# An attention and mixer kernel with every engine's order written out, conversions in thirds, and a tiny weight in place of a repair

## The chip, the cores and the metric

One core of one Trainium2 chip. The metric is device time in microseconds (us) of one execution. Ratios are the mean time of one kernel's fast runs over the mean of the other's of the same rounds, so they are not quite the ratio of the medians that are quoted.

Engines: PE is TensorE, DVE is VectorE, ACT is ScalarE, POOL is GpSimd. "L371" is line 371 of the kernel that a profile belongs to. "Half clock" is a stretch in which the trace shows a granted TensorE clock of 0.5; "the lock" or "the port" is what DVE and POOL share (the prediction shows it); a bank is a piece of the memory that PE writes its products to. Names in the profiles: hp is the product of the hash and g its bits, sc the scores, e their exps, esa and esd the sums of exps made by POOL and DVE, sums their total on PE, den the reciprocal, XT the output of attention, trp its transposes and x their copies, t the products of the token mixer.

## The reference

```python
# attention: batch 4, heads 8, sequence 768, head dimension 64; proj is 64 x 6
q_bits = (q @ proj > 0); k_bits = (k @ proj > 0)           # six bits each: a bucket
scores = where(bucket(q) == bucket(k), q @ k.T / 8, -1e9)
attn   = softmax(scores); x = attn @ v                      # heads joined: x is 4 x 768 x 512
# mixer; the four weights come as float64
h  = relu(x.T @ w_tok1) @ w_tok2 ; u = x + h.T              # over the sequence
h2 = relu(u @ w_ch1) @ w_ch2     ; out = u + h2             # over the channels
```
A query with no key in its bucket gets, by the softmax of equal scores, the mean of all values.

## The kernel before

The program has three parts: attention (16 pairs of heads, each in two halves of the queries), a token mixer and a channel mixer. PE's order is that of the source; the order of all other engines is chosen by a scheduler. PE adds the masking term by a second product of hash bits, so a query without equal keys gets exps of zero and a sum of zero, which is repaired after the sums.

```python
# conversion of 128 x 768 float64 words to float32: lo and hi are the two halves
raw = pool.tile([P, NW, 2], U32, ..., bufs=3); nc.sync.dma_start(out=raw, in_=src)
nc.vector.tensor_scalar(big, hi, 3, 0x3FFFFFFF, op0=shift_left, op1=and)          # L138
nc.vector.scalar_tensor_tensor(big, hi, 0xC0000000, big, op0=and, op1=or)         # L142
nc.vector.tensor_scalar(unit, big, 0xFF800000, None, op0=and)                     # L147
nc.vector.scalar_tensor_tensor(unit, lo, 2.0**-52, unit, op0=mult, op1=mult)      # L150
nc.gpsimd.tensor_tensor(big, big, unit, op=add)                                   # L151
nc.gpsimd.tensor_tensor(size, hi, hi, op=mult)                                    # L154
nc.vector.scalar_tensor_tensor(to, size, LEAST*LEAST, big, op0=is_ge, op1=mult)   # L155
# ...
def collect(es):                       # sum of the six exps of a half
    a = es[0] + es[1]; a = a + es[2]                 # POOL, L265, L266
    d = es[3] + es[4]; d = d + es[5]; d = d + a      # DVE, L268 to L270
def divide(n, half, num, es):
    # sums = ones @ es                                 PE, L278
    none = (sums == 0)                               # DVE, L280
    den = none * S + sums                            # DVE, L282
    den = 1 / den                                    # DVE, L285
    num = none * vsum + num                          # DVE, L286
    XT = num * den                                   # POOL, L290
# ...
for n, half, g in groups:
    es = scores(n, half, ...)                        # PE L232, ACT exp L249
    if held is not None: step(held)                  # weigh (PE L257), divide, collect
    if half == 0 and g == 0:
        load(n + 3); look(n + 1)                     # look: range read, DVE L195
    if half == 1 and g == 0 and n % 2 == 1: hashes(n + 1)   # for two pairs
    if weights and n >= 2 and half == 0 and g == 1: weights.pop(0)()   # one conversion
# token mixer: turn (transposes), mix1 (L440), mix2 (L452, adds into XT L458);
# 16 of the 20 conversions stand here, four before each batch
```

## Time and profile before

| | before |
|---|---|
| median of three runs | 1014.91 us |
| span of the profiled run | 1008.7 us |
| attention, from the first weighing's end to the first mixer product | 26.9 to 403.4 us |
| token mixer, to the first channel product | 403.4 to 508.9 us |
| channel mixer and end | 508.9 to 1008.7 us |

### The profile page before, as it was taken

How to read it: one execution, taken by the hardware profiler on the slowest of the kernel's cores; microseconds unless marked ns; L12 is line 12 of the kernel's file. 1: busy time of each engine (PE TensorE's matmuls, PEld its weight loads, DVE VectorE, ACT ScalarE, POOL GpSimd, SP SyncE). 2: the span in 40 equal slices, each digit the busy share in tenths (PEclk: the TensorE clock that was granted, in tenths of full speed). 3: DMA queues.
4: the chain of work that ended last, by engine and by line, in shares of the span. 5: the costliest groups of instructions: out<-in, count | busy, mean ns of one | idle time of the engine just before them, and what ended most of it. 6: DMA issues, size and time to landing. Idle time of an engine off the chain costs nothing.

```text
span 1008.7 us, 9010 instructions
## 1 busy us (share of the span) xinstructions
PE 943.9 (94%) x3649; PEld 423.4 (42%) x3649; DVE 400.3 (40%) x425; ACT 240.7 (24%) x361; POOL 223.6 (22%) x153
## 2 busy tenths in 40 slices
PE   5838999999999998989799999999999999999997
PEld 1313443444344344544444444444444444444443
DVE  2787778879787867566660000000000000000000
ACT  3404554554455455210011001001001101100100
POOL 4533533443344443444330000000000000000000
PEclk9968999999999999989899999999999999999999
DMA  6502221321121002223210000000000000000000
GB/s 231 209 1 67 79 98 34 98 81 63 66 63 52 18 2 94 95 94 94 94 32 0 21 21 1 20 22 0 11 21 10 1 31 11 0 21 21 1 11 33
DMA packets 16912, 48.52 MB, mean 48 GB/s; under 512 B 2080, under 2 KB 2528, under 8 KB 16864
## 3 DMA queue, kind: packets, MB, share of 16 engines
q1 hardware_dynamic: 16864, 47.88, 13.8%
q8 instruction: 30, 0.49, 0.2%
q14 instruction: 18, 0.15, 0.0%
HBM read 40.90 MB, written 6.29 MB: 47 GB/s over the span
## 4 chain that ended last, share of the span: by engine, by line
PE 69%; DVE 17%; POOL 6%; DMA 3%; issue 3%; ACT 2%; SPq 1%; DVEq 0%; POOLq 0%; ACTq 0%
PE c L466 25%; PE c L476 25%; PE sc L232 10%; PE acc L257 7%; POOL tmp L151 3%; POOL raw L154 2%; DVE den L285 2%; DVE tmp L150 2%; DMA qk<-in_qk 2%; DVE tmp L142 2%; ACT e L249 1%; DVE esd L269 1%; DVE esd L268 1%; PE sums L278 1%; PE hp L207 1%
## 5 line engine op out<-in xcount | busy, mean ns | idle before, releaser
L466 PE MATMUL c<-XT,WC 128*128 128x512 f32 x576 | 248.3, 592 | 0.6 <-DVE XT L458 0.6
L476 PE MATMUL c<-r,WC 128*128 128x512 f32 x576 | 248.2, 592 | 0.0
L480 DVE TENSOR_TENSOR o<-c,XT 128x512 f32<-128x512 f32 x24 | 16.6, 692 | 458.8 <-PE c L476 458.8
L249 ACT ACTIVATE e<-sc 128x768 f32<-128x768 f32 x192 | 151.9, 809 | 141.6 <-PE sc L232 141.1
L232 PE MATMUL sc<-qk 64*128 64x384 f32 x768 | 168.9, 519 | 0.6 <-ACT e L249 0.6
L466 PEld LDWEIGHTS c<-XT,WC 128*128 128x128 f32 x576 | 109.4, 190 | 138.4 <-issue 137.0
L476 PEld LDWEIGHTS c<-r,WC 128*128 128x128 f32 x576 | 109.4, 190 | 137.8 <-issue 137.8
L471 ACT ACTIVATE r<-c 128x512 f32<-128x512 f32 x72 | 43.0, 597 | 441.4 <-PE c L466 441.4
L257 PE MATMUL acc<-e,vn 128*64 128x384 f32 x768 | 137.9, 494 | 0.0
L265 POOL TENSOR_TENSOR esa<-e 128x768 f32<-128x768 f32 x32 | 59.2, 1851 | 181.2 <-ACT e L249 181.2
L232 PEld LDWEIGHTS sc<-qk 64*128 64x128 f32 x768 | 68.1, 194 | 71.5 <-issue 60.5
L257 PEld LDWEIGHTS acc<-e,vn 128*64 128x64 f32 x768 | 49.5, 136 | 76.4 <-issue 75.5
L285 DVE RECIPROCAL den<-den 128x384 f32<-128x384 f32 x32 | 81.5, 2545 | 0.0
L232 PE MATMUL sc<-bits 64*128 64x384 bf16 x384 | 65.4, 328 | 1.9 <-DMA bits<-g 1.9
L266 POOL TENSOR_TENSOR esa<-esa,e 128x768 f32<-128x768 f32 x32 | 60.8, 1901 | 0.1
L151 POOL TENSOR_TENSOR tmp<-tmp 128x768 f32<-128x768 f32 x20 | 36.7, 1836 | 89.8 <-DVE tmp L150 89.8
L268 DVE TENSOR_TENSOR esd<-e 128x768 f32<-128x768 f32 x32 | 39.1, 1223 | 33.5 <-ACT e L249 33.3
L207 PE MATMUL hp<-qk,projblk 128*32 128x384 f32 x128 | 19.0, 628 | 34.0 <-DVE g L211 14.9
L452 PE MATMUL t<-W,r 128*128 128x384 f32 x128 | 43.8, 501 | 7.5 <-DVE XT L458 7.5
L440 PE MATMUL t<-x,W 128*128 128x512 f32 x96 | 43.5, 610 | 0.6 <-DVE XT L458 0.6
L290 POOL TENSOR_TENSOR XT<-num,den 128x384 f32<-128x384 f32 x32 | 33.4, 1043 | 32.5 <-DVE den L285 29.5
L195 DVE TENSOR_REDUCE largest<-qk 128x1 f32<-128x1536 f32 x16 | 27.7, 1730 | 29.8 <-DMA qk<-in_qk 29.8
(46 smaller groups left out, 464.6 us busy)
## 6 DMA issues: line engine op xcount, KB each, us to landing
qk<-in_qk SPq DMA_DIRECT2D x16, 768.0 KB
raw<-in_moe_w_ch SPq DMA_DIRECT2D x16, 768.0 KB
vn<-in_v SPq DMA_DIRECT2D x16, 384.0 KB
vt<-in_vT SPq DMA_DIRECT2D x16, 384.0 KB
out<-o SPq DMA_DIRECT2D x24, 256.0 KB
raw<-in_moe_w_tok SPq DMA_DIRECT2D x4, 768.0 KB
bits<-g SPq DMA_DIRECT2D x64, 10.5 KB
projblk<-in_proj SPq DMA_DIRECT2D x2, 1.5 KB
```

The lines of the kernel that those rows point to most:

```text
L151: nc.gpsimd.tensor_tensor(big, big, unit, op=ALU.add)
L232: nc.tensor.matmul(sc[c][:, i, :HALF], t[rows, 1, P * c : P * c + P], t[rows, 0, qs], start=first, stop=not first,)
L249: nc.scalar.activation(e, sc[c][:, :, :HALF], ACT.Exp, scale=SCALE)
L257: nc.tensor.matmul(acc[D * i : D * i + D, :HALF], vn[:, i, c], e[:, i], start=(c == 0), stop=(c == NR - 1),)
L265: nc.gpsimd.tensor_tensor(a, es[0], es[1], op=ALU.add)
L266: nc.gpsimd.tensor_tensor(a, a, es[2], op=ALU.add)
L268: nc.vector.tensor_tensor(d, es[3], es[4], op=ALU.add)
L285: nc.vector.reciprocal(den, den)
L440: nc.tensor.matmul(ps, W1[:, r, P * j : P * j + P], x[:, r], start=(r == 0), stop=(r == NR - 1),)
L452: nc.tensor.matmul(ps[:, :HALF], r1[:, j, P * cb : P * cb + P], W2[:, j, HALF * half : HALF * half + HALF], start=(j == 0), stop=(j == NJ ...
L466: nc.tensor.matmul(ps, WC1[:, cb, P * t : P * t + P], XT[:, cb, sl], start=(cb == 0), stop=(cb == NCB - 1),)
L476: nc.tensor.matmul(ps, WC2[:, t, P * cb : P * cb + P], r2[t], start=(t == 0), stop=(t == NHT - 1),)
```

## The change

Its intent: PE shall not wait for DVE. The repair is gone: every key gets a weight of 2^-82 in the sums, by the values' sum in the copy of the weighed values and by a constant in the last add. The range read moves into the channel part. A conversion is cut in three pieces, one in each half. Two of its operations go to ACT. The order of all engines is that of the source.

```diff
 class Conversion:
+    def begin(self):                                  # first third
+        nc.scalar.activation(lo.bitcast(F32), lo, ACT.Copy, scale=2.0**-52)       # L162
         nc.vector.tensor_scalar(big, hi, 3, 0x3FFFFFFF, ...)                      # L164
         nc.vector.scalar_tensor_tensor(big, hi, 0xC0000000, big, ...)             # L167
+    def join(self):                                   # middle third
         nc.vector.tensor_scalar(unit, big, 0xFF800000, ...)                       # L179
-        nc.vector.scalar_tensor_tensor(unit, lo, 2.0**-52, unit, ...)
+        nc.scalar.activation(hi, hi, ACT.Square)                                  # L182
+        nc.gpsimd.tensor_tensor(unit, unit, lo, op=ALU.mult)                      # L183
         nc.gpsimd.tensor_tensor(big, big, unit, op=ALU.add)                       # L184
-        nc.gpsimd.tensor_tensor(size, hi, hi, op=ALU.mult)
+    def end(self):                                    # last third: DVE, L193
+    def one(self):  # mixer: begin and join of this conversion, end of the one before, next fetch

 def divide(...):
-    none = ...; den = ...; num = ...
+    nc.vector.reciprocal(den, ps[:, :HALF])                                       # L322

+for n in range(len(pairs)):
+    for half in range(2):
+        now.scores(0)
+        if before: before.weigh(1)
+        if half == 0:
+            load(n + 2)
+            if n + 1 < len(pairs): hashes(n + 1)       # DVE L265, L266
+        if before: before.add(0)                       # DVE L367, L368
+        now.scores(1)
+        if half == 0 and n + 1 < len(pairs): add_values(n + 1)
+        if n:
+            weights.some(third); third = (third + 1) % 3
+        now.weigh(0)                                   # POOL esa L355
+        if before: before.add(1); before.divide()      # DVE L370, L371; PE sums L320; POOL XT L324
+        before = now
+# 8 conversions in attention, 12 in the mixer:
 def mix1(b):
+    if b or not first: turn(b, x, banks)               # transposes L223, copies to x on ACT L224
     for j in range(NJ):
         ...                                            # products L513, relu on ACT L516
+        weights.one()
 def mix2(b):
     for cb in range(NCB):
         ...                                            # products L526, adds into XT on DVE L532
+        if cb % 2: weights.one()
+# bits buffers 4 -> 3, qk buffers 4 -> 3; mixer banks 8 -> 4, with two pairs of banks for transposes
```

## The prediction

> **What bounds the kernel now.** I read the page first, then who waited for whom on PE, then the timelines of PE, DVE and POOL, and the order in which the changed program's instructions stand on each engine.
>
> ```profile
> PE 943.9 (94%) x3649; PEld 423.4 (42%) x3649; DVE 400.3 (40%) x425; ACT 240.7 (24%) x361; POOL 223.6 (22%) x153
> ...
> PE   5838999999999998989799999999999999999997
> ...
> DVE  2787778879787867566660000000000000000000
> ```
> PE is the bound. From slice 20 on DVE is idle and PE full: that is the channel part.
>
> ```profile
> 508.94 41.47 PE c L466 x96
> 550.41 41.20 PE c L476 x96
> ```
> Twelve such pieces take 508.9 to 1003.6 us, 41.2 each, without a gap. The change cannot shorten them. All gain must come from the first 509 us.
>
> ```profile
> PE hp L207 <- DVE g L211: 14.9, 8, 5.1
> PE hp L207 <- DVE den L282: 10.6, 1, 10.6
> PE sums L278 <- DVE den L282: 8.3, 1, 8.3
> PE t L452 <- DVE XT L458: 7.5, 1, 7.5
> ```
> There PE waits for DVE: 8.3 + 10.6 + 5.1 us between 46 and 80 us, where the weight conversions stand ahead of the sums of exps in DVE's queue; some 9 us more at later hashes; 7.5 us in the token mixer, where 16 conversions hold up the adds into XT.
>
> ```profile
> 101.85 2.62 PE sc L232 x18
> 104.47 2.09 PE acc L257 x12
> 106.56 0.65 PE sums L278 x4
> 107.20 2.62 PE sc L232 x18
> 109.82 2.09 PE acc L257 x12
> 111.91 2.62 PE sc L232 x18
> ```
> Undisturbed, one half of a pair is 2 x (2.62 + 2.09) + 0.65 = 10.07 us of PE. There are 32 halves. A hash without its wait adds 0.78.
>
> **What the Trainium skill says.** "SBUF — State Buffer", section "Who interferes with whom": a DVE instruction with two SBUF inputs and a GpSimd instruction that reads SBUF exclude each other; the later one blocks until the other is done. The trace agrees:
>
> ```profile
> 335.52 0.96 DVE L268 TENSOR_TENSOR esd<-e 128x768 f32<-128x768 f32 x1
> 336.58 1.57 DVE L269 TENSOR_TENSOR esd<-esd,e 128x768 f32<-128x768 f32 x1
> ...
> 335.63 1.70 POOL L290 TENSOR_TENSOR XT<-num,den 128x384 f32<-128x384 f32 x1 [2.96 <-DVE den L285]
> 337.30 2.51 POOL L266 TENSOR_TENSOR esa<-esa,e 128x768 f32<-128x768 f32 x1
> ```
> Alone these take 0.96, 0.96, 1.00 and 1.81 us. Here they alternate: each waits out the one before.
>
> "TensorE: Matmul & The Clock Gate", section "What's actually happening": the clock falls to half after an idle window of about 3.4 us, and windows run freely. The trace agrees only in part: gaps of 2.26 us (at 166 and 255 us) already cost about 1.5 us of half-speed matmuls, one of 2.47 us (at 344) cost none, and gaps under 0.7 none.
>
> "DMA: Bandwidth & Descriptors", section "Queues, rings and completion order": a queue's descriptors are consumed in ring order. The trace fits: bits issued from 14.9 us land only after the big loads queued first, which keep the DMA busy to about 14.2 us.
>
> **The change, part by part.**
>
> Start. Now the first hash needs pair 0 alone (before: pairs 0 and 1, the second landing at 9.9 us). The hash ends near 7 us. The first bits follow 3.9 MB of loads in the same queue, and at the roughly 400 GB/s that the DMA moved early, they land near 13.5 us instead of 18.6. Behind them come, at the half clock seen there, 1.8 us of bits, 1.5 of the second hash, 4.2 of scores and 2.1 of weighing. The first weighing ends near 23.2 us; before, at 26.9. Gain 3.7.
>
> Attention from there. PE work: 31 halves x 10.07 = 312.2, plus 14 hashes x 0.78 = 10.9: 323.1. What is removed: the old waits (24 + 9) and some 7 us of half clock after them. DVE loses "none", the two repairs (0.55 + 0.55 + 0.61 to 0.8 per half, about 61 us in all by the page's means of lines 280, 282 and 286) and the 27.7 us of range reads. The third add of esa moves from POOL to DVE.
>
> But the written order makes a new wait. In the first half of each pair DVE has, in order: the hash's compare and scale, two adds, a third of a conversion, two adds, the reciprocal. PE has: scores, weighing, hash, scores, weighing, sums. The compare cannot start before the hash is done, so DVE sits idle from the end of the reciprocal (2.6 us into the half) to 5.6. From the hash's end PE needs 2.62 + 2.0 = 4.6 us to reach sums. DVE needs 0.56 + 0.3 + (1.06 + 0.88 + 1.06 + 0.96, the spacing seen at dependent and independent adds) = 4.8, and latencies. PE waits 0.6 us with no third, 1.9 with the first third (0.60 + 0.87 more), 1.3 with the last (0.9), 1.2 with the middle one. Thirds go round over pairs 1 to 12, so four of each: 4 x (1.9 + 1.3 + 1.2) + 2 x 0.6 = 18.8 us. This needs no lock.
>
> The lock adds to it. In a middle third POOL's multiply (1.8) gets between the last two adds, 1.2 more each; in second halves POOL's XT and esa go between DVE's adds from 2.6 us on, so sums come at 10.3 (first third) or 9.8 (last) instead of 9.3. Together up to 4 x (1.2 + 0.95 + 0.44) = 10.4 us. I take 7.2, since who gets the port first is a matter of tenths of a microsecond. Half clock after the longer of these gaps: eight of 1.9 us or more, a third of them at 1.5: 4. New waits: 18.8 + 7.2 + 4 = 30 us, against the 40 removed.
>
> End of attention. Weighing 2.1, the transposes of batch 0 2.6, a wait for the last sums 2.5 (DVE starts its four adds at 2.6 us, POOL's XT between, and ends at 7.2), sums 0.65; then the first mixer product takes the bank of the sums and waits for the reciprocal, 2.6. Together 10.5. From the end of the first weighing to the first mixer product: 323.1 + 30 + 10.5 = 363.6 us; before: 403.4 - 26.9 = 376.5.
>
> Token mixer. Eight products of 10.31 and three rounds of transposes of 2.62: 90.3. Only 12 conversions are left (8 of the old 20 went into attention), on DVE 0.57 + 0.96 + 0.57 + 0.96 = 3.1 us each instead of 4.1, and placed behind the adds. PE has four banks, so the 7.5 us wait should go. I allow 3 us of rest. 93.3 against 508.9 - 403.4 = 105.5. Conversions' copy and square go to ACT, which has 24% load: hidden.
>
> Channels. The 12.6 MB of range reads and 16 reductions of 1.73 us lie beside 41 us stretches in which DVE and DMA idle: hidden. The judge's transpose now waits for the last add before it: 1 us.
>
> **Sum.** Channel start: 23.2 + 363.6 + 93.3 = 480.1, before 508.9: -28.8. Plus 1 for the judge: -27.8. From the median: 1014.9 - 27.8 = 987.1 us.
>
> **Rivals.** (A) The order was tuned so that DVE is never late: new waits near 5 us. Then 30 - 5 = 25 us less: 962. For it: DVE's own work per half, about 7.3 us without a third, is less than 10.07. Against: the compare's place in the order, which I can read off the program. (B) The lock and the half clock strike fully: 10.4 instead of 7.2, 10 instead of 4, and in the mixer ACT waits for weight loads that must wait for attention's buffers: some 15 us more, 1002, which is within 2%. For it: 2.26 us gaps went cold twice. Against: the 2.47 us gap did not. (C) Range reads disturb the channel part, through DMA or DVE's order: up to some 10 us. Against: before, with outputs being written there, every piece stayed at 41.2; 12.6 MB over 400 us is 31 GB/s. I give it 5%.
>
> **Range and chances.** The sum says 987, just past the 2% line at 994.6. The firm part (start, mixer, 18.8 of new wait) may be off by 5 us either way; lock and clock are worth 10 us upward, a shorter chain 20 downward. 8 in 10: 968 to 1001. Faster by over 2%: 0.68, within 2%: 0.30, slower: 0.02.
>
> **What would show it.** PE's waits should name sums <- DVE esd, at the first halves, 1 to 2.5 us each, about 20 to 30 us in all, with the smallest ones in the last pairs, where no third is left; hp <- DVE should be nearly gone, and t <- DVE XT with it. First mixer product <- reciprocal once, about 2.6. Channels 41.2 each. First weighing done near 23 us. I am wrong if sums wait under 10 us in all (then rival A), if PE waits for DMA or ACT in steady attention, or if a channel piece grows.

## More of the kernel before

The stages are read from PE's timeline. Busy time by stage, in the view of windows (columns: stretch, its length, then busy us and instructions of PE, PEld, DVE, ACT and POOL, then the granted clock, DMA share, GB/s):

```profile
27.00:403.00 376.00, 339.12 (x2157) 149.06 (x2157) 299.08 (x281) 176.67 (x254) 161.50 (x102) 0.96 0.20 67
403.00:509.00 106.00, 94.16 (x280) 49.92 (x278) 65.00 (x95) 12.87 (x24) 42.43 (x27) 0.94 0.30 99
509.00:1009.00 500.00, 494.61 (x1152) 218.74 (x1152) 28.19 (x43) 42.98 (x72) 9.25 (x6) 1.00 0.04 13
```

PE is full in the last stage only. In the first two it lacks 37 and 12 us, and its clock is below 1. The prediction shows the waits that make this.

## The result

| | before | after |
|---|---|---|
| median | 1014.69 us (4 runs) | 1001.59 us (999.72 to 1003.09, 4 runs) |
| ratio | 1 | 0.987, 95% interval 0.9849 to 0.9891 |
| span of the profiled run | 1008.7 us | 1001.3 us |
| first weighing ends | 26.9 us | 24.2 us |
| first mixer product | 403.4 us | 393.2 us |
| first channel product | 508.9 us | 499.9 us |

This is the same by the 2% rule, and 14.5 us above the predicted 987.1, just outside the range. The lines of the page after that answer to those of before, engine totals first, then busy tenths in 40 slices:

```profile
PE 946.6 (95%) x3649; PEld 423.4 (42%) x3649; DVE 386.1 (39%) x349; ACT 278.2 (28%) x389; POOL 197.4 (20%) x119
...
PE   6998998999999997988999999999999999999997
...
DVE  1577777777777787477400030020002003000000
```
DVE lost 14 us in all (61 us of repair and 19 us of L150 went; an add for each half came, and lines that ran longer beside POOL), ACT gained 38. PE's busy time did not fall. The waits of PE after (columns: who waited for whom, us in all, times, longest):

```profile
PE sums L320 <- DVE esd L371: 26.7, 19, 2.6
PE trp L223 <- ACT x L224: 8.5, 3, 3.5
PE hp L261 <- DMA projblk<-in_proj: 5.2, 1, 5.2
PE sc L285 <- DMA bits<-g: 4.6, 1, 4.6
PE t L513 <- DVE den L322: 2.7, 1, 2.7
PE judge L573 <- DVE top L571: 0.9, 1, 0.9
```
The old waits (hash and sums for the denominators, second product for XT) are gone. Two new ones stand in their place: sums for the adds, and the transposes for ACT's copies. By stage, in the same columns as before:

```profile
24.00:393.00 369.00, 339.65 (x2138) 145.79 (x2136) 272.26 (x220) 194.55 (x265) 141.78 (x78) 0.98 0.23 79
393.00:500.00 107.00, 98.30 (x297) 54.19 (x298) 64.17 (x80) 32.97 (x41) 48.40 (x25) 0.92 0.20 67
500.00:1001.00 501.00, 494.69 (x1154) 218.47 (x1152) 45.70 (x44) 43.04 (x72) 0.00 (x0) 1.00 0.11 38
```
The mixer takes as long as before (107 against 106 us), at a lower clock (0.92 against 0.94). The channel part is as it was, with the range reads in it. The mixer's first products (24 matmuls for each batch) show where its clock was lost:

```profile
393.23 13.43 PE L513 MATMUL t<-x,W 128*128 128x512 f32 x24 [2.74 <-DVE den L322]
410.78 10.46 PE L513 MATMUL t<-x,W 128*128 128x512 f32 x24
438.59 11.18 PE L513 MATMUL t<-x,W 128*128 128x512 f32 x24
467.12 12.26 PE L513 MATMUL t<-x,W 128*128 128x512 f32 x24
```
The first, 3.0 us too long, follows the two waits at the end of attention (2.6 us for the last add, 2.7 us for the reciprocal). The third and fourth follow the long waits for ACT's copies; with the transposes just before them they lost 4.2 us.

**How the sums come late.** The chain of waits in a first half that carries a middle third (start us, us, what):

```profile
86.87 0.83 PE hp L261 x8
...
87.72 0.57 DVE g L265
...
88.31 0.32 DVE g L266
...
88.64 0.88 DVE esd L367
...
89.60 0.96 DVE esd L368
90.56 0.47 DVE tmp L179
91.03 0.88 DVE esd L370
...
92.00 2.42 DVE esd L371
...
94.56 0.89 PE sums L320 x4
```
PE needs 4.6 us from the hash to the sums and could start them at 92.4; DVE needs 6.9. The last add, L371, takes 2.42 us instead of 0.96, because POOL has the port, as POOL's timeline shows:

```profile
91.17 2.43 POOL L183 TENSOR_TENSOR tmp<-tmp,raw 128x768 f32<-128x768 f32 x1 [5.25 <-ACT e L302]
```

**How the transposes come late.** Timelines of DVE, POOL, ACT and PE at the end of the second product of batch 0 and in the transposes of batch 2:

```profile
431.60 0.56 DVE L532 TENSOR_TENSOR XT<-t,XT 128x384 f32<-128x384 f32 x1 [0.28 <-PE t L526]
432.08 1.86 DVE L164 TENSOR_SCALAR tmp<-raw 128x768 uint32<-128x768 uint32 x1
433.97 0.96 DVE L167 SCALAR_TENSOR_TENSOR tmp<-raw,tmp 128x768 uint32<-128x768 uint32 x1
...
431.70 1.82 POOL L184 TENSOR_TENSOR tmp<-tmp 128x768 f32<-128x768 f32 x1
...
434.97 0.92 ACT L182 ACTIVATE raw<-raw 128x768 f32<-128x768 f32 x1 [4.72 <-DVE tmp L167]
435.78 1.90 ACT L224 COPY x<-trp 128x1024 f32<-128x1024 f32 x2
...
431.40 1.91 PE L223 MATMUL trp<-ident,XT 128*128 128x128 f32 x16
436.82 1.97 PE L223 MATMUL trp<-ident,XT 128*128 128x128 f32 x8 [3.51 <-ACT x L224]
```
Read from the right end: the third group of transposes at 436.8 needs a bank that the first copy (435.78) frees. That copy stands behind the square (434.97) in ACT's order. The square overwrites the high words, so it must wait until DVE has read them (L167 at 433.97). L167 stands behind the last add into XT (431.60), which waits for PE's last product. So the copy of the next batch cannot start before the end of this batch's products and a conversion on top. ACT itself is idle 4.7 us of this. POOL is in this chain too: while its L184 ran, DVE's L164 took 1.86 us instead of the 0.55 of the conversion before.

### The profile page after: what moved, and what is told of

It reads as the page before. It is cut to its first block, busy times and chain, and to the rows that moved or that the text cites. A ratio compares the mean times of both kernels' runs of the same rounds, so it can differ in the third digit from the quotient of the medians.

```text
span 1001.3 us, 9101 instructions
## 1 busy us (share of the span) xinstructions
PE 946.6 (95%) x3649; PEld 423.4 (42%) x3649; DVE 386.1 (39%) x349; ACT 278.2 (28%) x389; POOL 197.4 (20%) x119
## 4 chain that ended last, share of the span: by engine, by line
PE 83%; DVE 12%; ACT 1%; issue 1%; DMA 1%; SPq 0%; DVEq 0%; ACTq 0%
PE c L552 25%; PE c L542 25%; PE sc L285 12%; PE acc L310 8%; PE t L513 5%; PE t L526 4%; PE sums L320 3%; DVE esd L371 3%; DVE den L322 2%; DVE esd L370 2%; DVE esd L368 2%; DVE tmp L164 1%; PE hp L261 1%; DVE tmp L167 1%; DVE esd L367 1%
## 5 line engine op out<-in xcount | busy, mean ns | idle before, releaser
L322 DVE RECIPROCAL den<-sums 128x384 f32<-128x384 f32 x32 | 81.9, 2558 | 47.8 <-PE sums L320 47.8
L324 POOL TENSOR_TENSOR XT<-num,den 128x384 f32<-128x384 f32 x32 | 40.7, 1272 | 197.0 <-ACT e L302 166.9
L355 POOL TENSOR_TENSOR esa<-e 128x768 f32<-128x768 f32 x32 | 66.4, 2076 | 19.3 <-ACT e L302 19.2
L183 POOL TENSOR_TENSOR tmp<-tmp,raw 128x768 f32<-128x768 f32 x20 | 44.0, 2202 | 68.7 <-ACT raw L162 32.4
L320 PE MATMUL sums<-esd,ones 128*64 128x384 f32 x128 | 27.5, 505 | 26.8 <-DVE esd L371 26.7
L513 PE MATMUL t<-x,W 128*128 128x512 f32 x96 | 47.3, 654 | 2.7 <-DVE den L322 2.7
L371 DVE SCALAR_TENSOR_TENSOR esd<-esd,esa 128x768 f32<-128x768 f32 x32 | 42.3, 1322 | 3.3
L184 POOL TENSOR_TENSOR tmp<-tmp 128x768 f32<-128x768 f32 x20 | 42.0, 2099 | 1.6
L368 DVE TENSOR_TENSOR esd<-esd,e 128x768 f32<-128x768 f32 x32 | 41.0, 1280 | 3.3
```

The lines of the kernel that those rows point to most:

```text
L320: nc.tensor.matmul(ps[D * i : D * i + D, :HALF], ones, total[:, i], start=True, stop=True)
L322: nc.vector.reciprocal(den, ps[:, :HALF])
L355: nc.gpsimd.tensor_tensor(self.a, self.es[0], self.es[1], op=ALU.add)
L368: nc.vector.tensor_tensor(self.d, self.d, es[5], op=ALU.add)
L371: nc.vector.scalar_tensor_tensor(self.d, self.d, NR * EPS, self.a, op0=ALU.add, op1=ALU.add,)
L513: nc.tensor.matmul(ps, W1[:, r, P * j : P * j + P], x[:, r], start=(r == 0), stop=(r == NR - 1),)
```

## The experiments

Twelve kernels ran. "After" in the table is the changed kernel's control run.

| label | edit | median us (low to high) | ratio to before (95%) |
|---|---|---|---|
| c0_after | none | 998.72 (997.81 to 1002.2) | 0.9853 (0.9827 to 0.9878) |
| e1_mix_even | conversions after blocks 0 and 2 | 995.65 (993.93 to 996.87) | 0.9808 (0.9791 to 0.9826) |
| e2_adds_first | adds before the hash on DVE | 976.26 (973.45 to 977.34) | 0.9615 (0.9593 to 0.9638) |
| e3_third_late | third after the last add | 976.79 (976.47 to 977.57) | 0.9631 (0.9615 to 0.9647) |
| e5_square_pool | square on POOL in the mixer | 1002.12 (1000.96 to 1002.6) | 0.9872 (0.9836 to 0.9909) |
| e6_one_block | one conversion per second product | 989.3 (987.97 to 991.99) | 0.9753 (0.9714 to 0.9792) |
| e7_three | e2, e3 and e6 together | 956.47 (956.42 to 957.65) | 0.9428 (0.9393 to 0.9462) |
| e8_start | first bits ahead of later loads | 996.93 (996.08 to 999.92) | 0.9831 (0.9792 to 0.987) |
| e9_best | e7 and four small edits | 950.79 (949.68 to 951.7) | 0.9372 (0.9357 to 0.9388) |
| e10_no_pool_third | POOL's part of a third left out | 989.81 (989.57 to 992.11) | 0.9764 (0.9748 to 0.978) |
| b1_no_range | before, without range reads | 1002.29 (1001.94 to 1003.5) | 0.9884 (0.9867 to 0.99) |
| b2_no_repair | before, without the repair | 1005.84 (1005.36 to 1006.4) | 0.9916 (0.99 to 0.9933) |

### The control

> The changed kernel again, as a yardstick for the others of this call. Both theories: 999 to 1004 us, ratio to the kernel before 0.985 to 0.990. PE waits about 26 us for esd, 8 to 9 us for ACT's copies of transposes.

998.7 us, sums waited 26.8 us and transposes 8.5, as expected. Its profiled span is 997.0 us, 4.3 less than that of the first result, with the same waits; the difference is mostly half clock (granted clock 0.985 against 0.981): its fourth first product of the mixer, after the same wait of 3.5 us, ran at full clock.

### Where the mixer's conversions stand

```diff
-                if cb % 2:
+                if cb % 2 == 0:
                     weights.one()
```

> Conversions of the second product stand after blocks 0 and 2 instead of 1 and 3. Theory 1 (what the prediction missed is ACT's order: the square waits for DVE, which waits for PE's products, and the copies of the next transposes stand behind it): PE's waits for ACT's copies fall from 8.5 us to about 1.4 (the first one stays), with some 4 us of half clock behind them; time 11 us less, about 990. Rival (PE waits because two banks for transposes are too few, wherever the conversion stands): the waits stay at 7 us or more and the time within 3 us of the changed kernel.

A miss in size: 3 us less than the control, and the copies' wait fell from 8.5 to 4.6 us only. DVE's L167 now runs while POOL holds the port (2.45 us instead of 0.96 in its timeline), so the second square of the batch still starts at 434.3 where the changed kernel has 435.0, and two waits of 0.5 us for XT came in. By itself this run does not decide between the square and too few banks. The next two do.

```diff
     def join(self):
-        nc.scalar.activation(hi, hi, ACT.Square)
         nc.gpsimd.tensor_tensor(unit, unit, lo, op=ALU.mult)
         nc.gpsimd.tensor_tensor(big, big, unit, op=ALU.add)
+        nc.gpsimd.tensor_tensor(hi, hi, hi, op=ALU.mult)      # in the mixer only
```

> The changed kernel, but in the mixer alone the square of the high words is made by POOL again, where it stood before; everything else in place. Theory 1 (the square, waiting on ACT for DVE, holds up the copies of the transposes): PE's wait for those copies falls from 8.5 us to under 1.5, half clock after them goes too, time 8 to 12 us below the changed kernel, about 988 to 991. Rival (two banks for the transposes are too few, whatever ACT does): waits of about 1.5 us per round remain, 4 us or more in all, time within 5 us of the changed kernel.

The wait did what the square theory says, but the time was a miss (1002.1 us, 988 to 991 expected):

```profile
PE t L529 <- DVE XT L535: 8.1, 3, 3.8
...
PE trp L226 <- ACT x L227: 1.1, 3, 0.7
```
The copies' wait fell from 8.5 to 1.1 us, so ACT's square held them up, and two banks cost only 0.2 us in each later round. But a new wait of 8.1 us took its place, PE for the adds into XT: POOL now has three operations in each conversion,

```profile
443.40 2.44 POOL L184 TENSOR_TENSOR tmp<-tmp,raw 128x768 f32<-128x768 f32 x1 [0.55 <-issue]
445.92 2.00 POOL L185 TENSOR_TENSOR tmp<-tmp 128x768 f32<-128x768 f32 x1
447.87 2.18 POOL L187 TENSOR_TENSOR raw<-raw 128x768 f32<-128x768 f32 x1
450.60 2.43 POOL L184 TENSOR_TENSOR tmp<-tmp,raw 128x768 f32<-128x768 f32 x1 [0.55 <-issue]
```
7.2 us each, one after the other with hardly a gap, and DVE's operations of the next conversion, which stand ahead of adds, wait for it. A wait for these adds (7.5 us) stood in the kernel before, where the square was on POOL as well.

```diff
-                if cb % 2:
+                if cb == 1:
                     weights.one()
```

> The changed kernel, but in the second product a conversion stands after block 1 alone, not after 1 and 3; what is left is converted after the last product. Theory 1: the square is done before the transposes, so PE's wait for the copies falls to the 1.4 us of the first round; time about 10 us below the changed kernel, 988 to 991. Rival as in the square's run: 4 us or more of wait remain.

As expected: 989.3 us, 9.4 less than the control of the other call (in ratios to before, 1.0% less). In the profiles, 7.6 us of the 9.9 lie in the mixer; the rest is an earlier start and less half clock in attention, which the edit does not touch. The copies' wait is 1.9 us, of which 1.46 belong to the first round, where a conversion still stands right ahead. ACT's timeline shows the square done three microseconds ahead of the copies:

```profile
425.40 0.94 ACT L182 ACTIVATE raw<-raw 128x768 f32<-128x768 f32 x1 [4.18 <-DVE tmp L167]
429.38 1.93 ACT L224 COPY x<-trp 128x1024 f32<-128x1024 f32 x2 [3.04 <-PE trp L223]
```
The copies now wait for the transposes, not the other way round. The conversions left over ran after the last product without a wait of PE.

### DVE's order in attention

```diff
-                if half == 0:
-                    load(n + 2)
-                    if n + 1 < len(pairs): hashes(n + 1)
                 if before: before.add(0)
+                if half == 0:
+                    load(n + 2)
+                    if n + 1 < len(pairs): hashes(n + 1)
```

> DVE's first two adds stand before the hash's compare. Theory (DVE idles 3 us for the hash): in the first halves of pairs sums wait 0 to 1 us instead of 0.4 to 2.2, total wait for esd from 26.7 to 8 to 12 us (about 3 of them second halves, 2.6 the last), half clock 5 to 7 us less; time about 981. Rival (the lock against POOL decides, order does not): the wait moves to the scale, total stays over 18 us, time over 993.

976.3 us, 22.5 less than the control; 981 was expected. Waits for the adds:

```profile
PE sums L320 <- DVE esd L371: 7.5, 13, 2.6
```
Of 7.5 us, 2.0 are left in first halves (21.3 in the control), 2.9 in second halves and 2.6 at the end. Nothing changed but the place of the hash's two operations in one engine's order, so DVE's idling for the hash is the cause, and the lock does not decide.

```diff
-                if n: weights.some(third); third = (third + 1) % 3
                 now.weigh(0)
-                if before: before.add(1); before.divide()
+                if before: before.add(1)
+                if n: weights.some(third); third = (third + 1) % 3
+                if before: before.divide()
```

> The third of a conversion stands after the last add, before the reciprocal. Theory: every first half waits 0.4 to 0.6 us, second halves none: total 5 to 8 us plus the 2.6 of the end, no gap long enough for half clock; time about 978 to 982. Rival (the conversion's load on DVE and POOL costs wherever it stands): waits of over 1 us remain in pairs 1 to 12, total over 15 us, time over 988.

976.8 us, 21.9 less. All 14 first halves with a hash wait 0.40 us, whatever third they carry; second halves wait nothing:

```profile
PE sums L320 <- DVE esd L371: 8.2, 15, 2.6
```
The same conversions cost nothing where DVE would have waited for the sums anyway. (e2 and e3 each take away most of the same wait, so their gains do not add.)

### The lock by itself

```diff
+            if self.bufs > 1:          # in attention POOL's two operations are left out
                 nc.gpsimd.tensor_tensor(unit, unit, lo, op=ALU.mult)
                 nc.gpsimd.tensor_tensor(big, big, unit, op=ALU.add)
```

> The changed kernel, but in attention POOL's two operations of a conversion are left out (the low bits of a part of the weights are lost on purpose, a few parts in ten million). Theory of the lock: only first halves with a middle third change, their gap falls from 2.2 to 1.15 us, with 1.7 us of half clock behind most of them; gaps with first and last thirds stay at 1.75 and 1.15; wait for esd 26.7 to 22.5, time 6 to 10 us less. Rival (DVE's own operations make the 2.2): the gap stays over 1.8, time within 2 us.

First halves with a middle third fell from 2.20 to 0.75 us, below the expected 1.15; the other gaps stayed (1.76, 1.15, 0.73). The same add as above, in DVE's timeline, and the wait behind it, in PE's:

```profile
91.26 0.96 DVE L372 SCALAR_TENSOR_TENSOR esd<-esd,esa 128x768 f32<-128x768 f32 x1
```
```profile
92.36 0.87 PE L321 MATMUL sums<-esd,ones 128*64 128x384 f32 x4 [0.74 <-DVE esd L372]
```
So the lock was worth 1.45 us in each of these four, a little more than the 1.2 that I gave it. Time fell by 8.9 us against the control (0.9% in ratios to before), though only 5.5 us of waits went (26.8 to 21.3): half clock behind those gaps went with them, three iterations of about 1.4 us each in the control's trace (one of 1.7 us came in behind another gap).

### The start

```diff
-        for n in range(2): load(n)      # qk, values of both pairs, then the first weights
         ...
-        weights = Conversion(...)
         hashes(0)
+        load_v(1)                       # values of pair 1
+        weights = Conversion(...)
```

> The changed kernel, but the values of pair 1 and the first weights are loaded after the first bits. Theory 2 (the bits come late because 1.6 MB of loads stand in the queue ahead of them): PE's wait for bits falls from 4.6-5.1 us to under 1, first weighing done about 4 us earlier, time 4 to 6 us less, about 994. Rival (the issue of eight small transfers and their landing alone take that long): wait stays over 3 us, time within 2 us.

The wait for bits fell from 5.1 to 1.4 us, but ACT's exps then came 2.0 us late (they stand behind ACT's issue of bits, a table load and the value sum), and the time is only 1 to 2 us lower: 996.9 against 998.7, in ratios 0.2%, within the intervals. The queue theory holds for the wait. Of the 3.7 us gained there 2.0 were given back; in the profiles the first weighing ends at 22.5 us, 2.6 us earlier.

### Three edits together, and the rest

> Three edits together: adds before the hash, thirds after the last add, one conversion per second product. If the three causes are separate: waits for esd 2.6 to 4 us, for the copies 1.4, time about 998.7 - 22 - 5 - 10 = 962 (958 to 967). If DVE and POOL are short of time in attention whatever the order, over 970.

956.5 us, a little better than the additive estimate of 962: in attention no gap is left before the end, and no iteration is longer than its work (10.07 us, 10.85 with a hash).

> The three edits of the 956 us kernel, with four small ones: the later loads behind the first bits, fewer issues on ACT and the value sums after the first scores, no conversion right before the second batch's transposes, and another bank for the first mixer product. Theory: start 4 to 5 us earlier, the bank's wait of 2.7 us gone, copies' wait 1.9 to 0.5: 946 to 951 us. If the starting loads only move the wait to the second pair, or the bank's wait stays: 951 to 955.

The four small edits: values of pair 1 and the weights after the first bits; only two of the first bits issued by ACT, and the first value sum after the first scores; no conversion after the second block of batch 0's first product; one unused bank tile ahead of the first. 950.8 us, the fastest here, 6.3% under before; in the profiles, 5.0 of the 5.9 us gained on e7 are the start. PE's waits that are left:

```profile
PE hp L268 <- DMA projblk<-in_proj: 5.5, 1, 5.5
PE t L525 <- DVE den L329: 2.7, 1, 2.7
PE sums L327 <- DVE esd L378: 2.6, 1, 2.6
PE sc L292 <- DMA bits<-g: 1.1, 2, 0.6
PE judge L586 <- DVE top L584: 0.9, 1, 0.9
PE trp L223 <- ACT x L224: 0.7, 3, 0.2
PE hp L268 <- DMA qk<-in_qk: 0.3, 1, 0.3
```
The unused tile did nothing, though the time lies in the range that counted on it: the first mixer product still waits 2.7 us for the last reciprocal. That it is the bank of the sums that makes it wait was argued, and this run does not bear it out; what makes it wait stays open.

### Two parts of the change alone, in the kernel before

```diff
-            nc.vector.tensor_reduce(largest[:, n : n + 1], t, AX.XY, ALU.max, ...)
+    nc.vector.memset(largest, 1.0)     # once, at the start
```

> The kernel before, without the 16 range reads on DVE (the flag is set from a constant; the results stay right). If this part of the change pays in the place where hashes waited for DVE: the later hash waits (9 us) halve, the early 24 us fall by some 4: time 6 to 10 us less, about 1005. If conversions alone made the waits: within 3 us of before.

12.4 us less, more than the 6 to 10 expected. The three early waits fell by 1.8 us in all, not by 4 (13.1, 7.4 and 1.8 us against 10.6, 8.3 and 5.1); the later hash waits halved, as expected. The hash waits together:

```profile
PE hp L205 <- DVE g L209: 6.5, 8, 1.8
```
from 14.9 us. Of these the six later ones fell from 9.0 to 4.1 us, and the half clock behind their gaps of over 2 us went.

```diff
-            none = ...; den = ...; num = ...
-            nc.vector.reciprocal(den, den)
+            nc.vector.reciprocal(den, ps[:, :HALF])
```
The last add also adds 2^-79, so that no sum is zero.

> The kernel before, without the zero-sum repair on DVE (queries with no equal key get zero on purpose where the reference has a mean). DVE loses about 60 us. If DVE's load stood before the hashes and sums: early waits from 24 to about 15, later hash waits from 9 to 3: time 12 to 18 us less, about 1000. If the order of conversions alone made the early waits: 4 to 8 us less.

8.8 us less, under the expected 12 to 18. The sums' early wait of 8.3 us went (1.5 us came in at the end of attention), the hash's stayed (11.2), hashes wait 5.5 instead of 14.9 us, but a new wait of 9.1 us for ACT's exps came, in the order that the scheduler then chose:

```profile
PE sc L232 <- ACT e L249: 9.1, 7, 3.5
```
So neither part needs the written order to gain some 10 us. The two gains need not add, since both come in part from the later hash waits. The changed kernel, which has both and more, gained 13 to 15; e7 shows what its own order gave back, 42 us.

## Why the prediction was wrong

The sum in the prediction, on the span of the profile (1008.7 - 27.8 = 980.9), against the profile after:

| term | predicted us | measured us | off by |
|---|---|---|---|
| first weighing ends | 23.2 | 24.2 | +1.0 |
| attention: PE work | 323.1 | 323.1 | 0 |
| attention: sums wait for adds | 18.8 + 7.2 | 24.1 | -1.9 |
| attention: half clock and restarts | 4 | 10.8 | +6.8 |
| end of attention | 10.5 | 11.1 | +0.6 |
| token mixer | 93.3 | 106.6 | +13.3 |
| channels and end, against before | +1.0 | +1.7 | +0.7 |

The waits in attention are those of PE's list without the last, 26.7 - 2.6. "Half clock and restarts" is what 30 iterations took beyond their work (10.07 us, 10.85 with a hash) and their gap; the work is taken as predicted, and e7's iterations, which have no gap, bear it out. The sum of the last column is 20.5; span and median differ since the profiled run was the slowest of its four.

**The step that failed** is the token mixer: "Conversions' copy and square go to ACT, which has 24% load: hidden", and with it "I allow 3 us of rest". The rest was 16.3 us: 8.5 of transposes waiting for ACT's copies, 4.2 of half clock behind these waits, 3.0 of half clock in the first product and 0.6 of small pieces. So ACT's order cost 12.7 us; the 3.0 us stand in the e6, e7 and e9 profiles too (2.3 to 3.0 us), whose copies hardly wait: they follow the two waits at the end of attention, which the prediction had, without half clock after them. The 24% (28% after) is a share of busy time: ACT is idle 4.7 us while it holds up PE. What I did not do for ACT is what I had done for DVE, to write down its order and what each operation in it waits for. e6 and e5 show the mechanism: with the square early, or on POOL, the wait goes (1.9 and 1.1 us left). The wait that I expected to go, of products for XT, did go; in e5 one of 8.1 us was back. None of the signs that the prediction named looked at ACT in the mixer, so the signs that it gave for the waits came true while the sum failed.

**The second term** is a size: half clock in attention. I took 4 us from "eight gaps of 1.9 us or more, a third of them at 1.5". Measured are four of the eight, at 1.7 us, 6.8 in all; and about 0.2 us with each gap, 4 us in all, which I had not counted. Of the 0.2 us, some 0.16 lie in the iteration that ends in the gap and 0.05 in the next; in e2 even gaps of 0.22 us cost it.

**Two slips that nearly cancelled.** The sum for the gaps does not follow from its own pieces: 0.6 us with 0.60 + 0.87 or with 0.9 more gives 2.1 and 1.5 us, not 1.9 and 1.3, and so 20.3 in all, not 18.8; the measured gap with no third is 0.4, which brings it back. And at the start the bits landed at 15.9 us, not near 13.5, but the scores took 3.2 us, not 4.2, so the first weighing was only 1.0 us late. The reading of queue order from the trace before was wrong: there the bits were issued at 14.9 us, when the loads were through (the DMA was 4% busy from 15 to 19 us), so nothing stood ahead of them. e8 is the run that shows the queue.

What was right: the compare's place in DVE's order and its cost. The gaps were 1.75, 1.15 and 2.20 us for the first, last and middle third and 0.4 with none, against 1.9, 1.3, 1.2 + 1.2 and 0.6. Second halves waited 0.73 us with a first third and nothing otherwise (0.95, 0.44). e2 and e3 confirm the cause, e10 the lock's share. The end of attention, the judge (0.9) and the channel part, with the range reads hidden in it (rival C did not come), were near enough. Rival A (a tuned order without new waits) is out by 24 us of waits. Rival B had the right size, 1002, and part of its reason: half clock in attention was near its 10 us (10.8 with the restarts), and ACT was late in the mixer. But the waits for the adds were not above the forecast (24.1), and it blamed weight loads for ACT's lateness: no wait of ACT for them shows in the mixer after.

## What to carry to other kernels

An in-order engine can be idle and still be late. When work is moved to an engine "with room", follow each moved operation: what does it wait for (here, an in-place write that waits for another engine's read), and what urgent operation stands behind it? In a written order, place optional work where the engine would wait anyway: the same thirds cost 22 us ahead of an add and nothing behind it. And count a gap of PE at more than its length: it may be followed by matmuls at half clock.

## What the Trainium skill lacked or had wrong

- "TensorE: Matmul & The Clock Gate", section "Why this matters for your kernels", asks for no PE-idle gaps over about 3 us. Here shorter ones cost: of the 24 gaps of 2.20 us before sums in six kernels with the changed order (the changed kernel, its control, e1, e5, e6, e8), 16 were followed by an iteration 1.7 us too long; of 28 gaps of 1.74 to 1.80 us (the same and e10), 3; of the 28 of 1.15 us, none.
- "SBUF — State Buffer", section "Who interferes with whom", says that whoever issues first gets the shared pair and the other blocks. It does not say who comes next: with both engines' queues full they took turns (DVE 0.96 and 1.57 us, POOL 1.70 and 2.51 us at 335 us before; 2.45 us instead of 0.96 for DVE's L167 in the mixer): each of these waited for one operation of the other engine.
- No page that I read warns of an in-place operation of one engine on what another engine still reads. ACT's square waited 17.9 us in four waits for DVE's L167, while ACT was 28% busy over the span.
